# Layer A's spread of a weight or a reciprocal: four products as one group of the plan, in four banks, instead of two groups of two

## The chip, the cores and the metric

The program runs on one core of one Trainium2 chip. The metric is device time in microseconds (us) of one execution; lower is better. Three timed runs of the kernel before gave 2244.37, 2245.67 and 2248.56 us, so the median is 2245.67 us.

## What is computed

Four residual layers, A, B, A, B, act on one activation of 2048 tokens by 1024 channels, with 32 heads of 32 channels. Layer B is ordinary softmax attention. Layer A is linear attention with a two-sided softmax as the feature map. The part of layer A that matters here:

```python
pq = einsum("bhsd,hdf->bhsf", q, w_phi)             # pk likewise
phi_q = concat([softmax(pq), softmax(-pq)])         # phi_k likewise
kv = einsum("bhsf,bhsd->bhfd", phi_k, v);  z = sum_s phi_k
num = einsum("bhqf,bhfd->bhqd", phi_q, kv)
den = einsum("bhqf,bhf->bhq", phi_q, z) + 1e-6
x = x + (num / den) @ wo
```

The two softmax denominators and `den` are one number for each token and head. The kernel keeps them compact, as rows of one tile, and copies a row over the 32 channels of its head when it multiplies with it. This copying is the "spread".

## The kernel before, in words

**Order of the work.** Nothing is issued as it is written. Every piece of work is an `Op` with an engine, a planned duration, its dependencies, its buffers and a priority. `Sched.run` (line 170) is a list scheduler: it simulates the engines, gives each free engine the ready piece of lowest priority whose buffers can be had, and so fixes the order of each engine's instructions. The chip then runs these orders with its own durations. Three things of the planner bear on the change:

- `draw = random.Random(TIE)` (line 171): each planned duration of a VectorE or TensorE piece is multiplied by a random factor between 0.99 and 1.01, drawn in the order in which the pieces are made. `TIE` is the seed. It changes nothing that is computed, only which of two near equal pieces comes first in the plan.
- `_alloc` (line 95) hands out all buffers of a piece at once or none. Buffers that are tied by `with_` are taken together. A class has a quota of live buffers (line 329): "mm" 4, "bc" 4, "num" 2, "cmp" 2, "ln" 2. All draw on the same eight PSUM banks, and a piece that does not get its banks is passed over for a later one that does.
- A change of `mode`, the way in which a piece divides TensorE's array ("c" four column tiles, "r" row tiles, "s" 32 by 32), is planned at 0.1 us (`SWITCH`, line 51).

**Layer A's queries** (`a_queries`, line 937). It is called for each of 4 chunks of 512 tokens and each half of the heads, in both A layers: 16 calls. A call projects four tiles (class "mm", 32 matmuls of mode "c" each, recorded on L530, the helper line of all four-column matmuls) and ScalarE takes two exponentials of each (L951). The sums over a head (L962) go through logarithm, subtraction and exponential into a weight; VectorE splits it into a high and a low bf16 part (L915, L916). `spread` copies the weight over four tiles in four banks (L931, lhsT `selb`), and VectorE multiplies each with one half of the features (L979). Numerators (L994, mode "s", copied out by ScalarE at L1002) and the denominator (L1009) follow; the reciprocal is split (L915, L916), spread again (L931, lhsT `selr`), and VectorE multiplies (L1020). `a_out` (line 1024) is the output projection; L1033 adds it to the residual. Then the layer norm for layer B starts (`layernorm`, line 623; its two banks of class "ln" are read by ScalarE at L666 and L668 and by VectorE at L669; L691 and L695 are its last two steps).

So there are 32 calls of `spread`, 128 products in all. A product contracts 32 partitions and fills a bank of 128 by 512. In `spread` (lines 921 to 935) a loop over `a in (0, 2)` makes two pieces of two products, each with two banks of class "bc" and a planned duration of `MM`, 0.2165 us (line 372).

**Layer B.** ScalarE's exponentials (L1273) of the scores (TensorE, L1257, mode "r") and the products with v and ones (L1305) fill most of the time. Projections of layer B, 512 wide, run in between. Where the plan has nothing for TensorE, it puts in filler matmuls (L1557).

Of the kernel before, what the change touches and what calls it, by code (L numbers as in the profile page):

```python
# [52 lines left out]
OVER = {"DVE": 0.085, "ACT": 0.012}  # L53
NEXT = {"DVE": 0.05, "ACT": 0.13}
RING = 0.5
TIE = 17
LOOK = 8


# [10 lines left out]
class Sched:  # L70
# [11 lines left out]
    def op(self, eng, dur, fn, deps=(), bufs=(), prio=0.0, lat=None, mode=None):  # L82
        o = Op(eng, dur, LAT[eng] if lat is None else lat, fn, tuple(bufs), prio, mode, len(self.ops))
        for d in deps:
            if d is not None:
                d.out.append(o)
                o.ndep += 1
        for b in o.bufs:
            b.left += 1
        if eng == "DVE" and any(b.kind == "ps" and b.banks in ([(7,)], [(6,)]) for b in o.bufs):  # L90
            o.ahead = EVAC
        self.ops.append(o)
        return o
# [76 lines left out]
    def run(self):  # L170
        draw = random.Random(TIE)
        for o in self.ops:
            if TIE and o.eng in ("DVE", "PE"):
                o.dur *= 1 + draw.uniform(-0.01, 0.01)
# [167 lines left out]
SIDE = (2, 4)  # L342
FEW = (((0, 1, 3), (0, 1, 2)), ((0, 1, 3), (0, 1, 2)))
WHOLE = 2
WK = (0.0, 1.5)
SLABD = (1, 3)
TOK = (0.0, 0.6, 0.61, 0.62)
# [24 lines left out]
MM = 0.2165  # L372
# [3 lines left out]
def kernel(  # L376
# [13 lines left out]
    _, S, D = A_x.shape  # L390
# [93 lines left out]
    op = sch.op  # L484

    def sb(cls, *dims, dt=BF16):
        n = 1
        for d in dims:
            n *= d
        b = Buf("sb", -(-n * (4 if dt == F32 else 2) // 64) * 64, cls)  # L490
        b.with_ = ()

        def v():
            ap = arena[:, b.at // 2:b.at // 2 + n * (2 if dt == F32 else 1)]
            if dt == F32:
                ap = ap.bitcast(F32)
            if len(dims) == 2:
                ap = ap.rearrange("p (a b) -> p a b", a=dims[0])
            elif len(dims) == 3:
                ap = ap.rearrange("p (a b c) -> p a b c", a=dims[0], b=dims[1])  # L500
            return ap

        return b, v

    def ps(cls, banks):
        b = Buf("ps", 0, cls, banks)

        def v():
            return psum[:, b.at[0] * C512:(b.at[-1] + 1) * C512]

        return b, v

    ANY = [(x,) for x in (7, 6, 5, 4, 3, 2, 1, 0)]
# [6 lines left out]
    def dma(prio, fn, deps=(), bufs=(), q="SP", kb=256, issue=0.55):  # L520
        return op(q, issue, fn, deps, bufs, prio, lat=2.0 + kb / 200.0)
# [205 lines left out]
    def fold_phi(col, wd_v, prio, use_pe):  # L727
        w_t = []
        if use_pe:
# [3 lines left out]
                           (), [nb], q="AQ", kb=1024, issue=0.7)])  # L733
            ld[0][0].slack = WK[0]
            ld.append([dma(-20.0, lambda i=i: nc.sync.dma_start(
# [3 lines left out]
            for o in ld[1]:  # L739
                o.slack = WK[1]  # L740
            for g in range(G):
# [179 lines left out]
    def spread(r_b, r_v, dep, prio, to):  # L921

        got = []
        for a in (0, 2):
            bufs = [ps("bc", ANY) for _ in range(2)]
            bufs[0][0].with_ = (bufs[1][0],)

            def fn(a=a, bufs=bufs):
                for k in range(2):
                    rows = slice(32 * (a + k), 32 * (a + k) + 32)  # L930
                    nc.tensor.matmul(bufs[k][1](), lhsT=to[rows, :], rhs=r_v()[rows, :],  # L931
                                     start=True, stop=True, tile_position=(32 * (a + k), 0))
            bm = op("PE", MM, fn, [dep], [bufs[0][0], bufs[1][0], r_b], prio, mode="r")
            got += [(b, v, bm) for b, v in bufs]
        return got

    def a_queries(c, hf, prio, wq_s, state, o_chunk, early=0.0):
# [40 lines left out]
        for a, (b_, v_, bm) in enumerate(spread(h_b, h_v, h, prio, selb)):  # L978
            ew.append(op("DVE", dve_us(512), lambda v_=v_, a=a: nc.vector.tensor_tensor(  # L979
                out=eq[a][1]()[:, 1, :], in0=eq[a][1]()[:, 1, :], in1=v_(), op=ALU.mult),  # L980
                [bm, tot[1]], [b_, eq[a][0]], prio))
# [37 lines left out]
        for a, (b_, v_, bm) in enumerate(spread(k_b, k_v, k, prio, selr)):  # L1019
            o_done[4 * hf + a] = op("DVE", dve_us(512), lambda v_=v_, a=a: nc.vector.tensor_tensor(  # L1020
                out=o_v()[:, 4 * hf + a, :], in0=nums[a][1](), in1=v_(), op=ALU.mult),
                [bm, nums[a][2]], [b_, nums[a][0], o_b], prio)
# [374 lines left out]
    for layer in range(2):  # L1397
# [116 lines left out]
        for i in range(G):  # L1514
            pr = p0 - 7 + 2 * i
            if last and i >= G - WHOLE:
                pass
# [5 lines left out]
        if not last:  # L1523
            r_b, r_v = sb("w2r", 2, D)
            ld = dma(p0 - 10, lambda r_v=r_v: nc.gpsimd.dma_start(out=r_v(), in_=B_o[:, 6:8, :]), (), [r_b], q="GQ", kb=512)
        adds = []
        for i in range(G):
            pr = p0 + 20 + i
            if last and i >= G - WHOLE:
                b_last(qc, i // 2, i % 2, pr - G, bo_s[i % 2], oTs[qc], TAIL, "ACT", None, 0, 4, [last_s])  # L1530
# [62 lines left out]
```

## Time and profile before

| | before |
|---|---|
| median of 3 runs | 2245.67 us (2244.37 to 2248.56) |
| the profiled execution | 2247.36 us |
| its span | 2245.1 us |
| mean granted TensorE clock | 0.998 |
| TensorE busy | 2176.1 us, 97% of the span |
| VectorE busy | 1855.9 us, 83% |
| ScalarE busy | 1985.7 us, 88% |
| GpSimd busy | 197.0 us, 9% |

The profile is that of one execution. Its span runs from the first to the last instruction, so 2.3 us of the 2247.36 us lie outside. Rows of a view begin with the time from the span's start where the view goes in order of time; then come the busy time, the engine, the source line and the operation, "out<-in" with partitions by elements, and the count. "[0.42 <-issue]" behind a row says that the engine stood idle for 0.42 us before, and that nothing the profile shows released it. PE is TensorE's matmul, PEld its weight load, DVE VectorE, ACT ScalarE. Each matmul has its own weight load, so the row of the loads tells when a group enters the array.

### The profile page before, as it was taken

The page shows a single profiled execution, that of the slowest core. Times are in us where ns is not written, and L with a number is a line of the kernel's source. Part 1 is how long each engine was busy: PE and PEld are TensorE (multiplying, and loading weights), DVE is VectorE, ACT ScalarE, POOL GpSimd, SP SyncE. Part 2 cuts the span into 40 slices and gives each one's busy share as a digit, 9 for nine tenths or more (in the row PEclk, how much of TensorE's full clock was granted, in tenths as well). Part 3 has the DMA queues.
Part 4 walks back from the last instruction along what each step waited for, and adds up shares of the span by engine and source line. Part 5 has one row for each costly group of instructions (what it writes and reads, how often), then busy time and mean ns, then how long its engine had stood idle before and what let it go on. Part 6 is the DMA issues. An engine that isn't in the chain of part 4 may idle for free.

```text
span 2245.1 us, 82636 instructions
## 1 busy us (share of the span) xinstructions
PE 2176.1 (97%) x36788; PEld 872.2 (39%) x36788; DVE 1855.9 (83%) x2761; ACT 1985.7 (88%) x1939; POOL 197.0 (9%) x299
## 2 busy tenths in 40 slices
PE   7999999999999999999999999999999999999999
PEld 4554454444333333333333444433333333333333
DVE  7986873698899889677887788799999999988968
ACT  4436669999999999999998555999999999999998
POOL 1110000000001010121124200000000000100000
PEclk9999999999999999999999999999999999999999
DMA  9220101111122221222235100111111100211111
GB/s 207 49 81 3 33 24 42 41 34 34 51 57 88 74 73 54 64 96 73 78 110 152 59 5 10 36 37 38 36 29 29 35 24 19 73 31 35 47 36 38
DMA packets 121789, 119.67 MB, mean 53 GB/s; under 512 B 57752, under 2 KB 99800, under 8 KB 121432
## 3 DMA queue, kind: packets, MB, share of 16 engines
q1 hardware_dynamic: 102392, 56.64, 10.0%
q0 software_dynamic: 17424, 56.18, 8.7%
q8 instruction: 287, 4.70, 0.9%
q10 hardware_dynamic: 1616, 1.57, 0.2%
q14 instruction: 70, 0.57, 0.1%
HBM read 79.23 MB, written 14.14 MB: 42 GB/s over the span
## 4 chain that ended last, share of the span: by engine, by line
PE 28%; ACT 23%; DVE 9%; issue 5%; DMA 1%; SPq 0%; ACTq 0%; DVEq 0%
ACT arena L1273 22%; PE psum L530 14%; PE psum L1305 6%; PE psum L1257 6%; DVE arena L1203 2%; DVE arena L1184 1%; DVE arena L1196 1%; DVE arena L1201 1%; DVE arena L1193 1%; ACT arena L823 1%; DMA arena<-arena 1%; DVE arena L1370 1%; DVE arena L1198 1%; DVE arena L1057 1%; PE psum L994 0%
## 5 line engine op out<-in xcount | busy, mean ns | idle before, releaser
L1273 ACT ACTIVATE arena<-psum 128x1536 bf16<-128x1536 f32 (+1 forms) x1366 | 1668.5, 1446 | 12.0 <-PE psum L1257 7.1
L530 PE MATMUL psum<-arena 128*32 128x512 bf16 (+1 forms) x18432 | 1058.3, 358 | 12.5 <-DVE arena L836 2.7
L530 PEld LDWEIGHTS <-arena 128*32 128x32 bf16 x18944 | 459.8, 96 | 447.2 <-issue 175.7
L1305 PE MATMUL psum<-arena 128*32 128x512 bf16 x4096 | 628.1, 383 | 4.0 <-issue 2.0
L1305 PE MATMUL psum<-arena,ones_bf 128*32 128x512 bf16 x4096 | 628.1, 383 | 0.0
L1257 PE MATMUL psum<-arena 32*128 32x512 bf16 x4096 | 536.2, 383 | 27.2 <-ACT arena L1273 22.4
L1257 PEld LDWEIGHTS <-arena 32*128 32x128 bf16 x4096 | 158.4, 91 | 555.8 <-issue 549.0
L1184 DVE TENSOR_SCALAR arena<-psum 128x512 int32<-128x512 f32 x418 | 284.5, 686 | 101.7 <-PE psum L1257 90.3
L1203 DVE SCALAR_TENSOR_TENSOR arena<-arena 128x1024 int16<-128x1024 int32 x209 | 254.7, 1218 | 5.7 <-DVE arena L1201 0.4
L1305 PEld LDWEIGHTS <-arena 128*32 128x32 bf16 x4096 | 163.2, 95 | 227.8 <-issue 177.0
L1305 PEld LDWEIGHTS <-ones_bf 128*32 128x32 bf16 x4096 | 161.3, 95 | 22.3 <-issue 7.9
L705 POOL DMA_DIRECT2D arena<-in_B_wqkv_dram x46 | 42.2, 919 | 1248.6 <-PE psum L530 302.5
L1193 DVE TENSOR_SCALAR arena<-arena 128x1024 f16<-128x1024 int16 x209 | 143.8, 690 | 4.4 <-DMA arena<-arena 0.3
L1196 DVE TENSOR_TENSOR arena<-arena 128x1024 f16<-128x1024 f16 x209 | 142.6, 684 | 4.6
L1201 DVE TENSOR_TENSOR arena<-arena 128x1024 f16<-128x1024 f16 x209 | 142.6, 684 | 3.1
L1057 DVE CAST arena<-psum 128x512 bf16<-128x512 f32 x128 | 87.7, 685 | 57.6 <-PE psum L530 57.3
L823 ACT ACTIVATE arena<-psum 128x512 bf16<-128x512 f32 x80 | 43.0, 596 | 82.6 <-PE psum L530 66.7
L827 DVE TENSOR_REDUCE arena<-arena 128x32 f32<-128x1024 bf16 x64 | 77.0, 1214 | 33.3 <-ACT arena L823 33.2
L530 PE MATMUL psum<-xT,onesD 128*32 128x512 bf16 x1144 | 103.1, 381 | 1.3 <-DVE arena L836 0.7
L1321 DVE COPY arena<-psum 128x512 f32<-128x512 f32 x126 | 86.3, 685 | 15.4 <-PE psum L1305 15.0
L1198 DVE TENSOR_SCALAR arena<-arena 128x1024 f16<-128x1024 f16 x209 | 87.9, 422 | 1.7
L836 DVE TENSOR_TENSOR arena<-psum,arena 128x1024 bf16<-128x1024 f32 x64 | 77.4, 1219 | 13.3 <-PE psum L530 9.7
(124 smaller groups left out, 1383.6 us busy)
## 6 DMA issues: line engine op xcount, KB each, us to landing
arena<-rd SPq DMA_DIRECT2D x62, 256.0 KB
arena<-in_B_wqkv_dram POOLq DMA_DIRECT2D x58, 256.0 KB, 4.1
arena<-in_B_wo_dram POOLq DMA_DIRECT2D x40, 256.0 KB, 4.4
arena<-arena SPq DMA_DIRECT2D x256, 32.0 KB
arena<-wd_k POOLq DMA_DIRECT2D x32, 256.0 KB, 5.0
arena<-in_A_wqkv_dram POOLq DMA_DIRECT2D x32, 256.0 KB, 4.6
arena<-arena SPq DMA_DIRECT2D x96, 64.0 KB
arena<-arena SPq DMA_DIRECT2D x248, 2.0 KB
```

The source lines that it names most:

```text
L530: nc.tensor.matmul(out_[ks, :], lhsT=lhsT[:, ks], rhs=rhs, start=start, stop=stop, tile_position=(0, 32 * k), skip_group_check=True)
L1057: return op("DVE", dve_us(512), lambda: nc.vector.tensor_copy(out=dst(), in_=src()), [dep], bufs, prio)
L1184: o = op("DVE", dve_us(512), lambda: nc.vector.tensor_scalar(out=x_v()[:, k, :].bitcast(I32), in0=s_v()[:, x * C512:(x + 1) * C512], scala ...
L1193: last = op("DVE", 1024 / 1920 + 0.15, lambda: nc.vector.tensor_scalar(out=z(), in0=x_v().bitcast(I16).rearrange("p a (n two) -> p a n two ...
L1196: last = op("DVE", 1024 / 1920 + 0.15, lambda: nc.vector.tensor_tensor(out=u(), in0=z(), in1=z(), op=ALU.mult), [last], [z_b, u_b], prio + ...
L1198: last = op("DVE", 1024 / 3840 + 0.15, lambda: nc.vector.tensor_scalar(out=u(), in0=u(), scalar1=POW2_C[0], scalar2=POW2_C[1], op0=ALU.mul ...
L1201: last = op("DVE", 1024 / 1920 + 0.15, lambda: nc.vector.tensor_tensor(out=u(), in0=z(), in1=u(), op=ALU.mult), [last], [z_b, u_b], prio + ...
L1203: return op("DVE", dve_us(1024), lambda: nc.vector.scalar_tensor_tensor(out=y_v().bitcast(I16), in0=x_v().bitcast(I32), scalar=128.0 / BIT ...
L1257: nc.tensor.matmul(out=s_v()[:, x * C512:(x + 1) * C512], lhsT=kT[g][1]()[r, pp, d * P:(d + 1) * P], rhs=q_of[(qc, g)][1]()[r, (pp + j // ...
L1273: ex = op("ACT", act_us(w * C512), lambda s_v=s_v, e_v=e_v, w=w: nc.scalar.activation(out=e_v(), in_=s_v()[:, 0:w * C512], func=ACT.Exp, s ...
L1305: nc.tensor.matmul(out=a_v()[col:col + 32, :], lhsT=v_v()[:, kc % 4, o:o + DH] if what == 0 else ones_bf[:], rhs=ev()[:, x * C512:(x + 1) ...
L1321: cp = op("DVE", dve_us(512), lambda t_v=t_v, a_v=a_v: nc.vector.tensor_copy(out=t_v(), in_=a_v()), [last], [a_b, t_b], prio - 4)
```

## The change

`spread` makes one piece of four products, with four banks that are allocated together, instead of two pieces of two. The planned duration of a piece stays `MM`, so a spread is planned at one `MM` instead of two. The seed of the planner's random factors goes from 17 to 14. The matmuls, their operands and everything behind them are the same.

```diff
-TIE = 17
+TIE = 14
...
+WIDEB = 4
...
     def spread(r_b, r_v, dep, prio, to):
 
         got = []
-        for a in (0, 2):
-            bufs = [ps("bc", ANY) for _ in range(2)]
-            bufs[0][0].with_ = (bufs[1][0],)
+        step = WIDEB
+        for a in range(0, 4, step):
+            bufs = [ps("bc", ANY) for _ in range(step)]
+            bufs[0][0].with_ = tuple(b for b, _ in bufs[1:])
 
             def fn(a=a, bufs=bufs):
-                for k in range(2):
+                for k in range(step):
                     rows = slice(32 * (a + k), 32 * (a + k) + 32)
                     nc.tensor.matmul(bufs[k][1](), lhsT=to[rows, :], rhs=r_v()[rows, :],
                                      start=True, stop=True, tile_position=(32 * (a + k), 0))
-            bm = op("PE", MM, fn, [dep], [bufs[0][0], bufs[1][0], r_b], prio, mode="r")
+            bm = op("PE", MM, fn, [dep], [*[b for b, _ in bufs], r_b], prio, mode="r")
             got += [(b, v, bm) for b, v in bufs]
         return got
```

## The prediction

> **What bounds the kernel now.** The page comes first: its span, and the slices of TensorE (PE) and ScalarE (ACT).
>
> ```profile
> span 2245.1 us, 82636 instructions
> ...
> PE   7999999999999999999999999999999999999999
> ...
> ACT  4436669999999999999998555999999999999998
> ```
>
> TensorE is full from the second slice on. ScalarE is full only in two long stretches: those are layer B's attention. In between, where its digits are 3 to 6, lies layer A. A spread exists only in layer A, so I ask the view of windows about the stretches from the first to the last spread of either layer (178.5 to 305, 1266 to 1388), the 40 us behind the first, and the two attentions. Columns: window, length, busy us of PE, PEld, DVE, ACT, POOL, clock, DMA.
>
> ```profile
> 178.50:305.00 126.50, 126.34 (x2346) 56.39 (x2342) 98.00 (x149) 82.98 (x147) 5.51 (x7) 1.00 0.07 19
> 305.00:345.00 40.00, 38.85 (x850) 22.58 (x848) 24.63 (x27) 26.18 (x34) 2.65 (x3) 1.00 0.13 33
> 345.00:1215.00 870.00, 847.52 (x13347) 308.60 (x13345) 687.96 (x1020) 861.41 (x731) 122.93 (x173) 1.00 0.25 69
> ...
> 1266.00:1388.00 122.00, 121.84 (x2278) 54.86 (x2270) 93.88 (x144) 79.14 (x142) 0.00 (x0) 1.00 0.02 5
> ...
> 1445.00:2245.00 800.00, 778.00 (x11784) 280.15 (x11776) 715.73 (x1114) 789.83 (x667) 21.38 (x25) 1.00 0.13 36
> ```
>
> In the two stretches with spreads TensorE is idle for 0.16 us each, while VectorE has 28.5 and 28.1 us to spare and ScalarE 43 us. TensorE's time is therefore the stage's time, provided that it does real work. The same windows, asked for the filler matmuls of L1557 alone, say that it does:
>
> ```profile
> 178.50:305.00 126.50, 0.00 (x0) 0.00 (x0) 1.00 0.07 19
> 1266.00:1388.00 122.00, 0.00 (x0) 0.00 (x0) 1.00 0.02 5
> ```
>
> So a microsecond of TensorE saved here moves everything behind it forward by about a microsecond, and a late VectorE or ScalarE costs only what TensorE cannot fill. In the attentions ScalarE is the bound, with 8.6 and 10.2 us of idle time.
>
> **What a spread costs now.** The view of line L931, cut to the weights `selb` and `selr`:
>
> ```profile
> L931 PE MATMUL psum<-arena,selb x64: 371/384/385, 178.6 to 1379.2; 32*128 32x512 bf16 x64
> ...
> L931 PE MATMUL psum<-arena,selr x64: 371/384/386, 186.4 to 1387.5; 32*128 32x512 bf16 x64
> ```
>
> That is 128 products of 384 ns. Two pieces in the plan need not be two blocks on the chip, so I read the timeline around each. The first spread, with its consumer, then the last:
>
> ```profile
> 178.57 0.10 PEld L931 LDWEIGHTS <-selb 32*128 32x128 bf16 x4 [0.42 <-issue]
> 178.57 0.39 PE L931 MATMUL psum<-arena,selb 32*128 32x512 bf16 x4
> 178.90 0.98 PEld L530 LDWEIGHTS <-arena 128*32 128x32 bf16 x24 [0.23 <-issue]
> ...
> 179.00 2.48 DVE L979 TENSOR_TENSOR arena<-arena,psum 128x512 bf16<-128x512 bf16 x4 [0.22 <-PE psum L931]
> ...
> 1387.47 0.10 PEld L931 LDWEIGHTS <-selr 32*128 32x128 bf16 x4 [0.42 <-issue]
> ```
>
> The two pieces already stand side by side: four weight loads, four matmuls within 0.39 us, and the next work enters 0.33 us after the first load. So it is in 29 of the 32 spreads; these two rows are the first and the last of the 29. **Most of what the change asks for has already happened.** Three spreads, all of the reciprocal, are in two blocks with projections between them:
>
> ```profile
> 263.71 0.58 ACT L668 COPY arena<-psum 128x512 f32<-128x512 f32 x1
> 263.85 0.69 DVE L669 TENSOR_TENSOR arena<-psum,arena 128x512 f32<-128x512 f32 x1 [0.85 <-ACT arena L666]
> 264.08 0.09 PEld L931 LDWEIGHTS <-selr 32*128 32x128 bf16 x2 [0.42 <-issue]
> ...
> 264.40 0.55 PEld L530 LDWEIGHTS <-arena 128*32 128x32 bf16 x16 [0.23 <-issue]
> ...
> 265.38 0.09 PEld L931 LDWEIGHTS <-selr 32*128 32x128 bf16 x2 [0.42 <-issue]
> ...
> 265.70 2.28 PEld L530 LDWEIGHTS <-arena 128*32 128x32 bf16 x48 [0.23 <-issue]
> ...
> 303.07 0.10 PEld L931 LDWEIGHTS <-selr 32*128 32x128 bf16 x2 [0.21 <-issue]
> ...
> 304.81 0.10 PEld L931 LDWEIGHTS <-selr 32*128 32x128 bf16 x2 [0.42 <-issue]
> ...
> 305.13 7.13 PE L530 MATMUL psum<-arena 128*32 128x512 bf16 x192
> ...
> 1351.04 0.09 PEld L931 LDWEIGHTS <-selr 32*128 32x128 bf16 x2 [0.42 <-issue]
> ```
>
> The reader should see three things. A block of two takes as long as one of four: 0.32 us from its first load (264.08) to the next work (264.40). Ahead of a block the loads stand idle for about 0.42 us, while matmuls of the other mode run out. And the first of the splits, at 264, falls where the layer norm's banks are still being read (L668 until 264.29, L669 until 264.54): two banks were free and two were not. The third split, at 1351.04 and 1352.34, looks the same.
>
> **Term 1, three blocks fewer.** What a needless block takes from TensorE: 0.10 us for the last load ahead of it (a load's own length in the rows), 0.42 us idle, and 0.32 us to the next work, 0.84 us in all, less the slot that one ordinary matmul has anyway. The chain of waits gives that slot:
>
> ```profile
> 1225.22 22.56 PE psum L530 x416
> ```
>
> 22.56 / 416 = 0.054 us. A block is 0.84 - 0.05 = 0.79 us, three of them **2.4 us**. The bounds: nothing, if the merged groups get waits of as much instead; 2.4 us if they get none.
>
> **Term 2, waits inside a block.** In some of the 29 the fourth product enters late, since its bank is still read by VectorE or ScalarE. The three longest:
>
> ```profile
> 216.31 0.09 PEld L931 LDWEIGHTS <-selb 32*128 32x128 bf16 x1 [0.33 <-issue]
> ...
> 293.06 0.09 PEld L931 LDWEIGHTS <-selb 32*128 32x128 bf16 x1 [0.33 <-issue]
> ...
> 1290.43 0.09 PEld L931 LDWEIGHTS <-selb 32*128 32x128 bf16 x1 [0.26 <-issue]
> ```
>
> They follow their block's start by 0.42, 0.42 and 0.35 us. All such waits together follow from the sum of L931's busy time over all windows:
>
> ```profile
> sum 2296.00, PE 15.49 PEld 4.17; mean PE 0.38 PEld 0.10
> ```
>
> 35 blocks (29 and 3 times 2) of 0.39 us would be 13.65 us; 15.49 is 1.8 us more. The planner allows the second piece its banks 0.22 us later than the first (the planned `MM`), but the chip runs the second right behind the first and stands. With one piece all four banks must be free at its planned start, so a wait should shrink by 0.22 us while projections run instead: the three above leave 0.2, 0.2 and 0.1 us, 0.5 to 0.6 together, and the short ones go. Bounds: 0 and 1.8 us; I take 1.8 - 0.6 = **1.2 us**. Terms 1 and 2 make 3.6 us.
>
> **What is moved or added.** No instruction is added or removed and no DMA; each matmul keeps its load. The new wait is that of the first two products for the third and fourth bank. Where four banks are free at once, 29 times of 32, it is nothing. In the other three the first pair moves back to where the second is, by 1.3 us (264.08 to 265.38), 1.7 and 1.3 us. Queued behind a spread are VectorE's four multiplications, and behind those numerators or the output projection. TensorE's cover is the 16 to 24 projections that ran between the pairs anyway; they now run ahead of the group. If that cover were gone, the three delays would cost 4.3 us.
>
> Four multiplications empty the four banks in 2.48 us (179.00), against 0.39 us for the products. The Trainium skill's page TensorEngine Tiling (Array Packing) says, in "PSUM Bottleneck", that tiling speeds TensorE but not the emptying of PSUM, which can then be the bottleneck, and, in "Gotcha 1: PSUM Pressure", that row tiles need different banks. By that rule the sum would be 0. The trace does not bear it out for the stage as a whole: VectorE has 28 us to spare in either stage, TensorE 0.16 (first windows).
>
> **Term 3, the redraw.** The new seed and 32 planned durations fewer shift every choice between near equal pieces, in all 2245 us. No row shows what that is worth, and its sign is open; I take 0 and bound it. Two layers are two draws on like work: 126.34 / 2346 = 53.9 ns per matmul against 121.84 / 2278 = 53.5, so 0.4 ns of 2300, 0.9 us for each A stage; idle shares of 0.99% (8.6 of 870) against 1.27% (10.2 of 800) in the attentions, so 0.28% of 835, 2.3 us each. All four on one side make 6.4 us, which is my estimate of its size. The far end below is all idle time of these stretches, 19 us; no reason puts an end above.
>
> **Sum.** The profiled execution is 2247.36 us; 3.6 less is 2243.8. It lies 1.7 us over the median of the runs; on the median, 2245.67 - 3.6 = **2242.1 us**. A measurement of this kernel can tell about 0.2% (4.5 us) from no change, so "same" is 2241.2 to 2250.2: the forecast lies near the edge.
>
> **The rivals.**
>
> *Starved of banks (slower).* With two banks free the old plan places a pair; the new one passes the spread over and gives the banks to later projections. Such a bank is held for 32 slots of 0.054 us and two exponentials, 1.7 + 1.2 = 2.9 us (two copies of 0.58, as L668's row has, for the 1.2). Turn after turn can do so, four with the quota of "mm", 11.6 us. It counts at the last spread of a layer, behind which everything waits for the output projection. The cover there is the 7.1 us of projections at 305.13; so it decides from 7.1 us of delay on, three turns. At four turns the price is 11.6 - 7.1 = 4.5 us a layer, 9 in both; less 3.6 makes +5.4, about **2251**. For it: the split at 303 is that last spread, and TensorE idles 1.15 us in the 40 us behind. Against it: 29 of 32 found four banks at once.
>
> *The redraw gains.* 3.6 and 6.4 together: **2236**. For it: idle time that a plan can avoid; against: it is 1% of the attentions.
>
> *The redraw loses.* 6.4 - 3.6 = 2.8 over the median: **2248.5**, or worse, as no row bounds it above. A good order has more ways to become worse than better.
>
> *Nothing is saved.* The blocks become fewer, but the stage goes at the pace at which VectorE empties the banks, 32 times 2.48 us before and after: **2245.7**. For it: the 2.48 us against 0.39; against it: VectorE's spare 28 us. The rule of the Trainium skill cited above would have it so.
>
> **How the numbers follow.** Forecast (2238 to 2246) 0.45, a little less than half of it under 2241.2; redraw gains (below 2238) 0.22; starved 0.15; redraw loses (2246 to 2256) 0.14; nothing saved 0.04. Faster is 0.22 and 0.20 of the forecast, 0.42. Same is its other 0.25, the 0.04 and 0.01 of the redraw's losses: 0.30. Slower is the rest, 0.28. The likeliest case's own range is 2238 to 2246. The range for 8 in 10 goes down to 2232 (the gaining redraw and about half of the 6.4 more) and up to 2255 (the starved case and nearly one layer's 4.5 more).
>
> **What would show it.** L931's loads in 32 rows of x4, none of x2, would show the change at work. Its busy time should fall from 15.49 to about 13.1 us (32 of 0.39 and 0.6 of waits); near 14.3 it would show that all waits stayed. The stretch from first to last spread, 126.2 us (178.57 to 304.81) and 120.9 us (1266.6 to 1387.5), should shorten by about 2 us each. Fillers or idle time of TensorE in these stretches would show starving. Where these hold and the total differs by more than 3 us from the forecast, the redraw did it, and then the attentions' ScalarE idle time (8.6 and 10.2 us) must have moved. I am wrong if a stage loses time although its groups are whole.

## The result, and the profile after

The changed kernel took 2252.97 us (median of 6 runs, 2250.81 to 2258.18) against 2245.44 us for the kernel before on the same chip: ratio 1.0037, 95% interval 1.0023 to 1.0051. It is 7.5 us slower, where 3.6 us faster was forecast. In a second comparison the same kernel had 1.0025 (1.0015 to 1.0035).

The spread itself came out as asked. In the changed kernel it is line L933. Its weight loads in the timeline, the first and the last of the 16 rows of the first layer (the second layer has as many):

```profile
183.57 0.10 PEld L933 LDWEIGHTS <-selb 32*128 32x128 bf16 x4 [0.42 <-issue]
...
307.00 0.10 PEld L933 LDWEIGHTS <-selr 32*128 32x128 bf16 x4 [0.42 <-issue]
```

And the sum of its busy time over all windows:

```profile
sum 2296.00, PE 12.63 PEld 3.39; mean PE 0.31 PEld 0.08
```

There are 32 blocks of four and none of two, and their busy time fell from 15.49 to 12.63 us; 13.1 was forecast. So the time was lost elsewhere. I cut the span at marks that both kernels have: the first spread of a layer (L931 or L933) and the first and last exponential of an attention (L1273 or L1275). The profiled executions took 2247.36 and 2253.35 us, with spans 5.6 us apart:

```
stretch (us)                               before   after   after, 2nd profile
start to first spread                      178.57  183.57   181.24
first spread to first exponential          148.58  147.51   147.53
first attention                            885.63  883.97   885.68
to the first spread of the second layer     53.84   55.34    57.38
first spread to first exponential          146.00  144.97   145.64
second attention                           822.36  823.89   822.96
to the end                                  10.17   11.45    11.46
```

The windows of the two stages that hold the spreads, before, then after. The columns are those of the prediction:

```profile
178.57:327.15 148.58, 148.43 (x2845) 69.83 (x2845) 114.97 (x168) 92.19 (x163) 6.39 (x8) 1.00 0.07 20
1266.62:1412.62 146.00, 145.84 (x2795) 69.17 (x2797) 114.69 (x168) 91.31 (x162) 2.68 (x3) 1.00 0.04 9
```

```profile
183.57:331.08 147.51, 147.13 (x2845) 69.31 (x2845) 114.96 (x168) 91.98 (x162) 6.38 (x8) 1.00 0.07 20
1270.40:1415.37 144.97, 144.97 (x2806) 72.37 (x2808) 114.76 (x168) 91.06 (x162) 2.66 (x3) 1.00 0.04 11
```

In the first stage both kernels run 2845 matmuls, so the figures can be compared: the stages are 1.1 and 1.0 us shorter. But **5.0 us are gone before the first spread has run** (2.7 in the second profile). The timeline of the changed kernel shows where. Row by row: seven loads of A's output weights are issued on GpSimd, 128 short matmuls follow, and then TensorE stands idle.

```profile
104.51 4.27 POOL L721 DMA_DIRECT2D arena<-in_A_wo_dram  x7
...
105.68 1.20 PE L857 MATMUL psum<-arena 128*32 128x33 bf16 x128
106.69 0.81 PEld L531 LDWEIGHTS <-arena 128*32 128x32 bf16 x19
...
110.86 0.61 PE L531 MATMUL psum<-phi_t,arena 128*32 128x128 bf16 x14 [3.06 <-issue]
110.86 0.55 PEld L531 LDWEIGHTS <-arena 128*32 128x32 bf16 x21 [3.35 <-issue]
...
112.01 0.25 PEld L531 LDWEIGHTS <-arena 128*32 128x32 bf16 x4 [0.18 <-issue]
```

The 3.06 us end in "issue": nothing that the profile shows released it. Behind it four loads take 0.43 us (0.25 and 0.18) instead of four slots of 0.054: a granted clock of one half, which the window shows as 0.82 of full over 3 us. The same windows of before and after:

```profile
109.00:112.00 3.00, 3.00 (x68) 1.66 (x62) 3.00 (x5) 0.52 (x1) 1.25 (x3) 1.00 0.97 322
```

```profile
109.00:112.00 3.00, 1.14 (x22) 0.80 (x25) 1.62 (x3) 0.50 (x1) 0.00 (x0) 0.82 1.02 348
```

In the kernel before, the same work passes without a wait:

```profile
105.99 4.26 POOL L720 DMA_DIRECT2D arena<-in_A_wo_dram  x7
...
107.35 1.31 PE L856 MATMUL psum<-arena 128*32 128x33 bf16 x128
108.47 2.98 PEld L530 LDWEIGHTS <-arena 128*32 128x32 bf16 x84
```

What the idle time waits for is in the trace's DMA packets. Two queues carry instructions; the packets of this one fit TensorE's count:

```profile
q8 instruction: 287, 4.70, 0.9%
```

287 packets of 16 KB for TensorE's 73,656 matmuls and loads: one packet holds 256 of them. From the trace, for the packet that matters in each run, when it was read and how many of TensorE's instructions had begun by then:

```
run               packet read at   begun    loads issued at   idle behind
before                105.51        4271        105.99           none
after                 108.42        4545        104.51           3.06
after, 2nd profile    107.12        4545        103.76           2.53
```

Before, the packet went just ahead of the loads. After, the loads were issued first and the packet was read 3.4 to 3.9 us behind them. The burst of 128 short matmuls (256 instructions in 1.2 us, where 128 matmuls of 512 columns with their loads take 6.9) would have used up what was fetched. The theory for the experiments, **Theory I**: a plan drawn anew lets TensorE run out of instructions, and the groups of four are not at fault. **Theory II**: the groups of four cost the time.

### The profile page after: what moved, and what is told of

The parts are those of the page before. It is cut to its first block, busy times and chain, and to the rows that moved or that the text cites. A ratio compares the mean times of both kernels' runs of the same rounds, so it can differ in the third digit from the quotient of the medians.

```text
span 2250.7 us, 82705 instructions
## 1 busy us (share of the span) xinstructions
PE 2171.7 (96%) x36828; PEld 874.2 (39%) x36828; DVE 1856.7 (82%) x2761; ACT 1986.6 (88%) x1939; POOL 200.1 (9%) x299
## 4 chain that ended last, share of the span: by engine, by line
PE 29%; ACT 18%; DVE 9%; issue 5%; DMA 1%; SPq 0%; ACTq 0%; DVEq 0%
ACT arena L1275 17%; PE psum L531 14%; PE psum L1307 7%; PE psum L1259 6%; DVE arena L1205 2%; DVE arena L1198 1%; DVE arena L1186 1%; DVE arena L1203 1%; DVE arena L1195 1%; ACT arena L824 1%; DMA arena<-arena 1%; DVE arena L1372 1%; DVE arena L1200 1%; DVE arena L1059 1%; DVE arena L696 0%
## 5 line engine op out<-in xcount | busy, mean ns | idle before, releaser
L1275 ACT ACTIVATE arena<-psum 128x1536 bf16<-128x1536 f32 (+1 forms) x1366 | 1668.4, 1426 | 10.3 <-PE psum L1259 5.3
L531 PEld LDWEIGHTS <-arena 128*32 128x32 bf16 x18944 | 465.8, 96 | 449.2 <-issue 181.2
L1307 PEld LDWEIGHTS <-arena 128*32 128x32 bf16 x4096 | 165.2, 95 | 225.2 <-issue 173.5
```

What stands on the lines that cost most here:

```text
L531: nc.tensor.matmul(out_[ks, :], lhsT=lhsT[:, ks], rhs=rhs, start=start, stop=stop, tile_position=(0, 32 * k), skip_group_check=True)
L1275: ex = op("ACT", act_us(w * C512), lambda s_v=s_v, e_v=e_v, w=w: nc.scalar.activation(out=e_v(), in_=s_v()[:, 0:w * C512], func=ACT.Exp, s ...
L1307: nc.tensor.matmul(out=a_v()[col:col + 32, :], lhsT=v_v()[:, kc % 4, o:o + DH] if what == 0 else ones_bf[:], rhs=ev()[:, x * C512:(x + 1) ...
```

## The experiments

All changes are to the kernel before unless it is said that they are to the changed one. A ratio is that to the kernel before on the same chip.

### Shifting the instruction stream of the changed kernel

```diff
+    for _ in range(8):
+        mm(psum[:, 7 * C512:7 * C512 + P], onesD[:], onesD[:], True, True, True)
     for o in sch.run():
         o.fn()
```

Each `mm` makes four matmuls, so these are 32.

> The changed kernel with 32 matmuls more at the start of TensorE's program (while it waits for its first data), which shift its whole instruction stream by 64 instructions and leave the plan as it is. Theory I (the loss is a place where TensorE runs out of fetched instructions, 3.06 us idle at 107.8 us, and the 3.4 us of half clock behind it): the idle time goes or shrinks below 1 us, no half clock near 110 us, and the median falls by 3 to 5 us from 2253.0, to 2248 to 2250. Theory II (the four-bank groups cost the time): the idle time stays and the median stays at 2252 to 2254.

Measured: 2250.22 us, ratio 1.0020 (1.0011 to 1.0030). The packet is read at 107.45 us with 4304 begun, behind loads issued at 106.80, and the idle time shrinks to 0.78 us:

```profile
106.80 4.28 POOL L721 DMA_DIRECT2D arena<-in_A_wo_dram  x7
...
109.83 0.27 PE L857 MATMUL psum<-arena 128*32 128x33 bf16 x14 [0.78 <-issue]
```

The half clock near 110 us is gone as well. TensorE had the same plan and the same groups, so the trace speaks for Theory I. The total speaks less clearly: 2250.22 us lies just above the 2248 to 2250 that I expected, and the interval of the ratio overlaps that of the unshifted kernel. The first spread came only 0.75 us earlier (182.82): at 100 us TensorE was already 2.3 us later than without the added matmuls. The shift had moved other fetches into its way: this profile has idle times of 1.02 us at 50.83 and of 1.48 us at 93.75, both "issue", which the unshifted one has not.

### The seed alone

```diff
-TIE = 17
+TIE = 14
```

> The kernel before with the seed 14 alone, pairs as before. Theory I (the redrawn plan sets the time, not the groups): the time differs from before by more than 2 us, either way, and the stretches from first to last spread stay at 125 to 127 us and 120 to 122 us. Theory II (the groups of four cost it): within 2 us of before, 2243 to 2248.

> The seed 14 with pairs, beside the run above. Theory I (in the two A stages the groups of four save 1 to 3 us and nothing else of theirs costs): 0 to 3 us slower than after_again. Theory II (the groups of four cost time outside the A stages, as the first ratios of 1.0037 and 1.0012 would have it): 3 to 7 us faster than after_again. First spread at 182 to 185 us by either, as the plan up to it is the same.

> The changed kernel once more, beside its own seed with pairs on the same chip, and for a second profile. Theory I (TensorE runs out of fetched instructions near 108 us, a property of the early plan and its DMAs): idle time over 1.5 us between 105 and 112 us again, first spread at 182 to 185 us. Theory III (the stall was chance of one execution): no such idle time, first spread near 179.

Measured: 2249.84 us, 1.0012 (1.0002 to 1.0021), and 2249.17 us, 1.0013 (1.0004 to 1.0023). So the seed alone, with pairs, costs 3 us. Its first spread is at 183.90 and 181.51 us, and it has the idle time too (2.29 us at 108.99, 2.02 at 108.67). TensorE's first 4034 matmuls, the first spread among them, are the same in the same order in this kernel and in the changed one. In its A stages the pairs need

```profile
183.90:332.73 148.83, 148.66 (x2845) 69.74 (x2845) 114.88 (x168) 91.94 (x162) 6.41 (x8) 1.00 0.07 20
...
1268.49:1414.42 145.93, 145.70 (x2797) 69.16 (x2797) 114.80 (x169) 91.70 (x161) 5.29 (x7) 1.00 0.06 16
```

against 147.51 and 144.97 for four: at one seed, the groups save 1.3 and 1.0 us (in the second profile 1.3 and 0.3; its second stage begins in a half clock). Yet the changed kernel beside it had 2252.71 us, 1.0025 (1.0015 to 1.0035), 3.5 us more. Theory I had expected the seed with pairs to be the slower one; that the groups cost 3 to 7 us outside the A stages was Theory II, and the total came out as it said. The stretch that holds the difference lies between: to the first spread of the second layer the pairs take 51.81 and 51.71 us, the changed kernel 55.34 and 57.38. There the same thing happens a second time, in both profiles of the changed kernel and in neither of the seed with pairs: loads, 128 short matmuls, idle time (1.78 us; 2.31 in the second profile).

```profile
1263.77 2.82 POOL L710 DMA_DIRECT2D arena<-in_B_wqkv_dram  x4
...
1264.43 1.27 PE L857 MATMUL psum<-arena 128*32 128x33 bf16 x128
...
1268.78 1.69 PE L531 MATMUL psum<-arena 128*32 128x512 bf16 x26 [1.78 <-issue]
```

With the stream shifted by 64 instructions the same groups in the same plan have no idle time there, and the stretch took 52.90 us. So it is not the groups as such that cost time there. Theory I holds, but wider than I had it: the place near 108 us comes with the seed, the one at 1267 us with the plan of the groups.

### The same loss without any change of plan

The kernel before, with 96 or with 128 matmuls at the start as above (`range(24)`, `range(32)`).

> The kernel before with 96 matmuls more at the start of TensorE's program, while it waits for its first data: 192 instructions, so the places where a block of 256 is fetched come 64 instructions later in the work. Plan, groups and seed are those of before. Theory I (the loss of the changed kernel is instruction fetch behind the weight loads): the fetch that began at 105.5 us, just ahead of the loads of 106.0, now comes behind them; idle time over 1.5 us between 105 and 112 us, first spread at 181 to 184 us, time 2 to 6 us over before. Theory II (the groups of four cost): nothing changes here, time within 2 us of before.

> The control: 128 matmuls more at the start, 256 instructions, one whole block, so every fetch falls where it fell before. Theory I: no idle time over 1 us between 105 and 112 us, first spread within 1 us of 178.6, time within 2 us of before. If the added matmuls themselves cost, both this and the kernel with 96 are slower by the same.

Measured: with 96, 2255.37 us, 1.0034 (1.0023 to 1.0046); with 128, 2248.06 us, 1.0007 (0.9994 to 1.0020). The kernel before with 96:

```profile
107.78 4.26 POOL L720 DMA_DIRECT2D arena<-in_A_wo_dram  x7
...
109.13 1.23 PE L856 MATMUL psum<-arena 128*32 128x33 bf16 x128
...
114.27 0.72 PE L530 MATMUL psum<-phi_t,arena 128*32 128x128 bf16 x22 [3.74 <-issue]
```

The idle time is there, 3.74 us, with the half clock behind it. The packet was read at 111.59 us with 4801 instructions begun: 4545 and one block of 256. The first spread came at 189.07 us instead of 178.57, and the time is 9.3 us over before; both are more than I had expected, since the start lost time elsewhere too (idle for 3.39 us at 9.59, where before has 2.81; a half clock at 66.6; idle for 1.95 us at 184.86). From first to last spread it takes 126.24 and 120.87 us, as before. **Pairs, seed 17, the old order: this shift alone costs as much as the change did.** The control is not quite clean: no idle time over 1 us up to 112 us and no measurable loss, but one of 2.98 us at 113.23 (5057 begun, another 256) and a first spread 2.1 us late.

A count over the traces goes further than these places. The 14 profiles together have 50 idle times of TensorE of 1 us or more that end in "issue". At every one the number of its instructions begun by then leaves a remainder of 193 or 194 when it is divided by 256 (4545 is 17 blocks of 256 and 193). Of the 74 other idle times of that length, which the profile ascribes to an engine or a DMA, one does. A wait for data would not keep to the count of instructions; a fetch in blocks of 256 does. And in all 50 TensorE goes on 2.2 to 3.1 us after an instruction packet was read.

Data traffic is not needed for such a wait, but the long ones have it. In the 2 us ahead of 16 of the 50 the data queues moved under 6 GB/s, and none of these is longer than 1.97 us; each one over 2 us comes behind 140 to 320 GB/s. That the loads hold the packet up is argued from this and from the order of issue; no run leaves the loads out. These idle times also differ between executions of one kernel: the second profile of the changed kernel has one of 1.41 us at 1250.32, the first has none there.

### The groups of four at seed 17

```diff
+WIDEB = 4
...
-        for a in (0, 2):
+        step = WIDEB
+        for a in range(0, 4, step):
```

The second of the next two kernels has besides

```diff
+                if o.bufs and o.bufs[0].cls == "bc" and len(o.bufs) > 4:
+                    draw.uniform(-0.01, 0.01)
...
-            bm = op("PE", MM, fn, [dep], [*[b for b, _ in bufs], r_b], prio, mode="r")
+            bm = op("PE", 2 * MM, fn, [dep], [*[b for b, _ in bufs], r_b], prio, mode="r")
```

> The groups of four with the seed 17; the draws of all later pieces shift by one for each spread, so this is a redrawn plan too. Theory I: no idle time of 3 us at 107.8 us unless by chance, stretches of about 123.4 and 119.4 us as in the changed kernel, time within 2240 to 2250. Theory II: 2250 to 2256 as the changed kernel.

> The groups of four with seed 17, two factors drawn for each group and a planned duration of two MM, so that every other piece keeps the factor that it had before and the plan is told the same TensorE time. What differs in the plan is only that four banks are asked for at once. Theory I: the first spread starts where it did (178.6 us, within 0.5), the two stretches are 1 to 4 us shorter than 126.2 and 120.9, the time is 2240 to 2246. Theory II: the stretches are as long as before or longer, 2248 to 2255.

Measured: 2257.27 us, 1.0048 (1.0031 to 1.0065), and 2252.76 us, 1.0034 (1.0022 to 1.0046). My theory missed both. Theory II had 2250 to 2256 for the first and 2248 to 2255 for the second, and the first stage is indeed longer than before (148.58) in both:

```profile
179.34:331.66 152.32, 149.90 (x2913) 72.42 (x2909) 113.26 (x166) 91.95 (x163) 6.39 (x8) 1.00 0.07 20
```

```profile
180.77:333.42 152.65, 150.59 (x2913) 73.74 (x2909) 112.97 (x166) 91.91 (x163) 6.39 (x8) 1.00 0.07 20
```

It is 3.7 and 4.1 us longer, with 2.4 and 2.1 us of idle TensorE and 68 matmuls more ahead of the first exponential. The second stages are 1.5 and 0.7 us shorter. The rest is no stage with groups: the first kernel spends 7.1 us more in the first attention (892.73), which I did not follow, and the second comes to its first spread 2.2 us late, in the order of before, with 1.40 us of idle TensorE at 124.03 (5313 begun, a remainder of 193 again). The timeline of the second kernel around the last spread (L935) of the first layer:

```profile
302.10 0.75 DVE L919 SCALAR_TENSOR_TENSOR arena<-arena,hl 128x512 bf16<-128x512 bf16 x1
...
302.75 9.13 PEld L533 LDWEIGHTS <-arena 128*32 128x32 bf16 x273 [0.23 <-issue]
...
314.75 2.80 PE L533 MATMUL psum<-arena 128*32 128x256 bf16 x96 [0.51 <-ACT arena L1060]
...
317.48 0.09 PEld L935 LDWEIGHTS <-selr 32*128 32x128 bf16 x2 [0.21 <-issue]
...
318.02 0.09 PEld L935 LDWEIGHTS <-selr 32*128 32x128 bf16 x2 [0.45 <-issue]
```

The split reciprocal is ready at 302.85 us. Its four products begin at 317.48, 14.6 us later, behind 400 matmuls of projections, which need banks one at a time and which the planner put ahead of it. In the kernel before, the two pairs (303.07 and 304.81) ran 2.3 and 4.0 us behind their reciprocal. This is the rival "starved of banks", at the place and with the delay that it was given. At seed 14 it does not occur: the changed kernel's spreads follow within 1.9 us, but for the first of the second layer, which stands behind the idle time at 1267 us (2.5 us, 3.9 in the second profile).

So Theory II holds for a starved stage; in the other stages the groups save. **Theory IV**: four banks at once save up to about 1.5 us in a stage (0.3 to 1.5 so far), unless one spread at its edge is starved, which costs about 4.

### Four banks only in the second A layer

```diff
-        step = WIDEB
+        step = WIDEB if layer else 2
```

with the same factors and `MM * step / 2`.

> Pairs in the first A layer, groups of four in the second, seed 17 with the factors of before. TensorE's order is that of before up to the second A layer. Theory IV (at seed 17 the groups of four lose by the starved last spread of the first A layer, 14.6 us behind its weight, about 4 us): time within 2 us of before, the second stretch 1 to 2 us shorter than 120.9. Theory II (groups of four cost wherever they stand): 3 us or more slower than before.

Measured: 2244.90 us, 0.9997 (0.9988 to 1.0007), as expected. The second stage:

```profile
1264.47:1409.97 145.50, 145.32 (x2799) 72.48 (x2801) 114.61 (x168) 92.10 (x162) 1.79 (x2) 1.00 0.04 9
```

From first to last spread it is 1.9 us shorter (118.97 against 120.86), of which the work behind the last spread takes 1.4 back (26.53 against 25.14). A gain of half a microsecond is all that reaches the attention.

### Four banks everywhere but in the starved spread

```diff
+        spreads.append(to)
+        step = 2 if len(spreads) == 16 else WIDEB
```

> Groups of four everywhere, seed 17 with the factors of before, but the last spread of the first A layer (the 16th of 32) in two pairs. Theory IV (that one spread, starved of a fourth bank, is what the groups of four lose at this seed): its products follow its weight within 5 us instead of 14.6, the time from the first spread to the first exponential of the attention falls from 152.6 to 147 to 148 us, the second layer's stays at 144.5 to 145.6, and the time is 2242 to 2247. If another spread is starved in its place, the first figure stays above 150.

Measured: 2257.48 us, 1.0047 (1.0033 to 1.0061). The first stage is mended (148.36 us, the products 2.2 and 3.9 us behind their weight), though a little longer than I expected, and the time is 10 us above the 2242 to 2247 that I expected. For the plan of all that follows changed, and in the second layer the first spread (L938) is starved in its place: ready at 1254.34, run at 1270.91.

```profile
1253.60 0.74 DVE L919 SCALAR_TENSOR_TENSOR arena<-arena,hl 128x512 bf16<-128x512 bf16 x1
...
1270.91 0.10 PEld L938 LDWEIGHTS <-selb 32*128 32x128 bf16 x4 [0.42 <-issue]
```

```profile
1270.91:1422.36 151.45, 150.65 (x3001) 76.45 (x3001) 118.46 (x176) 93.98 (x165) 4.96 (x7) 1.00 0.06 16
```

That stage now has 3001 matmuls and 151.45 us, 5.5 more than before; most of the rest of the loss lies ahead of the first spread (2.3 us) and in the first attention (2.5). The mechanism was right; taking it away at one place brought it up at another.

### Pairs and fours without random factors

`TIE = 0`, once in the kernel before, once in the changed one.

> The kernel before without random factors (seed 0), pairs. It is the partner of the next run. No theory gives its time beyond 2240 to 2260; its stretches from first to last spread should be 125 to 127 and 120 to 122 us.

> The changed kernel without random factors, groups of four. Same early plan as its partner. Theory IV (groups of four save 1 to 3 us in the A stages where the last spread of the first layer gets its banks, and lose about 4 where it is starved): first spread to first exponential of the attention 1 to 2 us shorter than the partner's if its last spread follows its weight within 3 us, 3 to 5 us longer if it follows after 10 us or more. Theory II: 3 us or more slower than the partner in either case.

Measured: 2254.33 us, 1.0030 (1.0018 to 1.0043), with pairs, and 2258.53 us, 1.0040 (1.0025 to 1.0056), with fours; the two ratios do not differ beyond their intervals. The last spread of the first layer waits 13.8 us with fours, and the stages are:

```profile
180.06:328.90 148.84, 148.73 (x2845) 70.26 (x2845) 114.70 (x168) 92.48 (x163) 6.40 (x8) 1.00 0.07 20
1274.93:1420.95 146.02, 145.91 (x2797) 68.75 (x2797) 114.80 (x169) 92.01 (x162) 4.63 (x6) 1.00 0.06 16
```

```profile
177.96:330.28 152.32, 149.90 (x2913) 72.53 (x2909) 113.26 (x166) 92.06 (x163) 6.39 (x8) 1.00 0.07 20
1271.50:1415.96 144.46, 144.46 (x2797) 67.80 (x2797) 115.80 (x169) 92.40 (x162) 5.49 (x7) 1.00 0.07 18
```

3.5 us longer in the starved stage, 1.6 us shorter in the other: Theory IV in kind and size once more. The pairs also show what a seed is worth: 2254.3 us against 2246.1, of which the first attention makes 6.3 us (891.93 against 885.63); why it is longer I did not follow.

No version measurably beats the kernel before; the closest is four banks in the second layer only.

## Why the prediction was wrong, point by point

**The bound of the stages** was right. The pairs' stages are the same at three seeds (148.58, 148.83, 148.84 us; 146.00, 145.93, 146.02), so TensorE's work sets them.

**Terms 1 and 2** (3.6 us) were right in kind and too large. At one seed the stages became 1.3 and 1.0 us shorter (1.3 and 0.3 in the second profile). From first to last spread it is 2.8 and 1.5 us less than before, but part of that is work that moved behind the last spread, where the path to the first exponential takes 1.7 and 0.5 us more. L931's busy time was right within 0.5 us.

**The starved rival** was right in its mechanism, its place (the last spread of a layer), its delay (11.6 us were worked out, 13.8 to 14.6 measured) and its price (4.5 us a layer; 3.5 to 4.1), but not in what spoke against it. "29 of 32 found four banks at once" said nothing of the one spread that matters, which was among the three exceptions. The changed kernel itself escaped it, so that the rival's 2251 lies near the measured 2252.97 is luck. The rival that came true is that of the redraw that loses (2248.5, or worse).

**Term 3 failed.** "No row shows what that is worth, and its sign is open; I take 0": the changed kernel lost 8 to 10 us here (7.5 and 6.4 in the medians of the two comparisons, and the 2.1 and 1.4 that the stages saved against before), and the mechanism was in the trace. Near 108 us idle time and half clock cost about 4.7 us in the profiled execution, 4.1 in the second (counted by matmuls begun, the first is 0.3 us behind before at 80 us and 5.0 at 120). The seed alone costs 3 us in the medians. The second place, at 1267 us, and a cause that I did not find (1.0 us after the last exponential, in both profiles against both of the seed with pairs) are seen in the rest. The kernel before has such places itself, idle for 1.97 us at 921.98 and 1.70 at 1147.26, both "issue" and both with a half clock behind. I read the total idle time of the stretches as something a plan might save, and did not ask what those waits were. The 6.4 us were added up from the two A stages and the two attentions; the start, the stretch between the layers and the end, where the changed kernel lost 5.0, 1.5 and 1.3 us, were not in the sum. For the two other seeds with pairs, 3 and 7 to 8 us slower, the size was about right and the middle was not; for the changed kernel it was too small as well. The sign that I had named for a redraw, ScalarE's idle time in the attentions, moved the other way: 6.0 and 8.2 us in the same windows, instead of 8.6 and 10.2.

**What stays open**: how much of the 3.5 us between the changed kernel and its seed with pairs is the fetch at 1267 us (its idle time is 1.78 and 2.31 us, while the stretch is 3.5 and 5.7 longer, with 2.3 and 1.6 back in the A stages), what makes the end 1 us longer, and what lengthens the first attention by 6 to 7 us in two of the plans.

## What to carry to other kernels

When a schedule is computed, a small edit changes all of it. Price the edit at a fixed plan and the new plan by itself, and run the seed alone as a control. A wait that the profile ascribes to nothing ("issue") on a full engine deserves a look at the instruction queue: here a burst of 128 short matmuls behind seven loads used up what was fetched, and 64 instructions more at the start moved the place. Count the instructions begun before each such wait: the same remainder at all of them, when divided by the size of a fetched block, points to the fetch. An allocation of all or nothing, under a planner that passes over whom it cannot serve, is judged by the one request at the edge of a stage, not by the share of requests that go through.

## What the runs showed of the hardware that was not expected

TensorE's instructions arrive in packets of 256, and an idle time stands where the fetched ones end: at 4545 instructions begun in the changed kernel's two profiles, at 4801 and 5057 with 96 and 128 matmuls more, 256 apart, and at one remainder in all 50 cases of the 14 profiles. The Trainium skill's page Runtime: NRT & Kernel Launch, section "Instruction fetch mechanics", has the blocks of 256 instructions and calls the cost of crossing into the next "mostly hidden". The trace agrees on the block and not on the cost: 2.0 to 3.7 us at one fetch near 110 us, when the packet is read behind data loads (220 to 370 GB/s in these windows). The idle time can also cost a second time: behind 16 of the 50, of 1.3 to 3.7 us each, the granted clock was one half for 3.4 us, which is 1.7 us of work. Behind the other 34 it was not, one of 2.98 us among them (113.23 us, 128 matmuls more), so the length of the idle time alone does not decide it.
